# Inputs asked for three units ahead, the routing bias ahead of them, and the last tile scaled on ScalarE

## The chip, the cores and the metric

The kernel runs on one core of a Trainium2 chip. The metric is the device time of one execution in microseconds (us). Before the change the median of three runs is 327.57 us (327.46 to 328.42).

## What is computed

Two stages follow each other: a linear attention with decay (RWKV) over 4 sequences of 768 steps with 8 heads of 48, and on its output a mixture of 8 experts that sends each of the 3072 rows to the one expert with the highest gate.

```python
for t in range(S):                       # attention, per batch and head
    cur = einsum('bhd,bhe->bhde', u * kt, vt)
    y[:, :, t] = einsum('bhd,bhde->bhe', rt, state + cur)
    state = wt[..., None] * state + einsum('bhd,bhe->bhde', kt, vt)

x = y as [3072, 384]                     # mixture of experts
logits = x @ w_gate + modality_bias[modality_id]
e = argmax(logits); gate = softmax(logits)[e]
out[row] = gate * (relu(x[row] @ w1[e]) @ w2[e])
```

## The kernel before, in words

The 3072 steps are cut into 24 units of 128 steps. The loop `for i in range(-2, NU)` (L1044) is a software pipeline over them: iteration `i` of `att_iter` (L400) prepares unit `a = i+2` (decay scans and the scaling of keys and receptances on VectorE), multiplies unit `m = i+1` (scores, key turn, state update on TensorE) and writes the output of unit `z = i`. GpSimd works one unit further ahead: in iteration `i` it makes the decays, the products r*k and the within-unit products (`decays`, `keys`, `within`, L320 to L337) of unit `i+3`, and then a share of `dV` of unit `i`. From iteration 15 on it also sends one finished row tile an iteration to the buffer `xs` in device memory (`scatter`, L834).

The inputs r, k, w of a unit lie in one of `NIN = 4` tiles `ins[n % 4]` (L106). `load(n, cuts, key)` (L130) asks for parts of unit n on SyncE's queue: k is the cut (512, 1024), w the cut (1024, LIN), r the cut (0, 512), of 256, 264 and 256 KB. With a key, the request also waits for the VectorE instruction recorded under it in `step`: ("second", i) is the second scan of iteration `i`, ("mask", i) the masking of the scores, ("first", i) the first scan. Before the change iteration `i` asks for unit `i+6` (L1071 to L1075). That unit goes into the tile of unit `i+2`, which the same iteration is still reading: k waits until VectorE has scaled the keys, w for the second scan, r until VectorE has scaled the receptances. After that comes `loadv(i + 3)`, which waits for the masking.

SyncE's queue is worked off in the order of the program. In iterations 18 to 23 it also holds zero fills of `xs` (`fill`, 386 KB each) and sixteen pieces of 192 KB of the first expert's weights (`w_raw` in parts of eight, EARLY); these are issued ahead of the unit requests of the same iteration. In iteration 0, `early()` (L215) asks for the routing's bias `bb` and the modality numbers `mi`; VectorE reads `bb` in `setup_a` (L230), which runs at the end of iteration 1. At the end of iteration 20 `blk_load(0)` (L856) asks for the rows of the first expert block in `xs`; it may only start when the scatters of units 0 to 5 have landed, of which the last is issued by GpSimd in iteration 20.

The expert stage then runs six blocks over TensorE (`blk_up`, `blk_down`). In the last block, tiles of 128 rows are scaled by the gate in `last_scale` (L962) and sent to the output by `last_out` (L970); the last tile is scaled by VectorE (L966), the one before by ScalarE (L968).

Of the kernel before, what the change touches and what calls it, by code (L numbers as in the profile page):

```python
# [13 lines left out]
AF = mybir.ActivationFunctionType  # L14
ALU = mybir.AluOpType
# [3 lines left out]
P = 128  # L19
# [3 lines left out]
DM = H * D  # L23
# [12 lines left out]
BT = WIDTH[-1]  # L36
# [19 lines left out]
LIN = 2 * 4 * P + WIN  # L56
# [26 lines left out]
def kernel(ctx: ExitStack, tc: tile.TileContext, rkw, vt, wf, cst, mid, wg, bias, w1, w2, out):  # L83
    nc = tc.nc
# [17 lines left out]
    BOTH = slice(0, 1), slice(1, 2)  # L102
    PREP = ("K", "G")
    WORK = ("R", "A", "W", "dT", "v", "wx")
    NIN = 4
    ins = [pa.tile([P, WO + WIN], F32, name=f"in{i}", bufs=1) for i in range(NIN)]  # L106
    pw = [pa.tile([P, 4 * SEG], F32, name=f"pw{i}", bufs=1) for i in range(NPW)]
    KT = wk.tile([P, 2, 4, 64], F32, name="KT", bufs=1)
    T = {}

    def wt(n, tag, sh, bufs=None, dt=F32):
        T[tag, n] = (pa if tag in PREP else wk if tag in WORK else rt).tile(sh, dt, tag=tag, name=f"{tag}{n}", bufs=bufs)
        return T[tag, n]
# [5 lines left out]
    step = {}  # L119
# [5 lines left out]
    def behind(dma, key):  # L125

        if key in step:
            after(dma, step[key])

    def load(n, cuts=((0, 512), (512, LIN)), key=None):  # L130
        for c0, c1 in cuts:
            o = KO - 512 if c0 else RO
            behind(nc.sync.dma_start(out=ins[n % NIN][:, o + c0:o + c1], in_=rkw[n, :, c0:c1]), key)

    def r_of(n):
        return ins[n % NIN][:, RO:RO + 512]

    def k_of(n):
        return ins[n % NIN][:, KO:KO + 512]

    def w_of(n):
        return ins[n % NIN][:, WO:WO + WIN].rearrange("p (a c b) -> p a c b", a=4, c=2)[:, :, :, 0:P // 2]

    def loadv(n, key=None):
        behind(nc.sync.dma_start(out=wt(n, "v", [P, DM], 4), in_=vt[n * P:(n + 1) * P, :]), key)
# [120 lines left out]
    def fill(j):  # L266
        n = BW // P // len(FILL)
        r = DUMMY + j * n * P
        ins = nc.sync.dma_start(out=xs[r:r + n * P, :].rearrange("(j p) c -> p j c", p=P), in_=zt[:, None, :].to_broadcast([P, n, XW]))
        rows_apart("xs", ins)  # L270
        return ins
# [59 lines left out]
    def within(n, *parts):  # L331
        t, o, l = ins[n % NIN], RO + P // 2, KO - RO - P // 2
        if n in APARTS and ("wx", n) not in T:
            wt(n, "wx", [P, 2, 4, P // 2], 2)
        for ks in parts:
            v = t[:, o:o + 2 * l].rearrange("p (k x) -> p k x", k=2)[:, ks, 0:512 - P // 2].rearrange("p k (c j) -> p k c j", j=P // 2)[:, :, ::2]
            nc.gpsimd.tensor_tensor(out=T["wx", n][:, ks] if n in APARTS else v, in0=v, in1=w_of(n).rearrange("p a k j -> p k a j")[:, ks], op=ALU.mult)  # L337
# [6 lines left out]
    def spread(n, tag, src, c0, bufs=None):  # L344
        X = sides(wt(n, tag, [P, 4, P], bufs).rearrange("p a b -> p (a b)"))
        be, k, v = heads(BE1 if (n, tag) == (1, "K") else BE)[:, :, c0:c0 + P // 2], 1 if tag == "K" else 0, sides(src)
        if n == 0 or n in APARTS:
            w = T["wx", n][:, k] if n else sides((r_of, k_of)[k](NIN - 1))[:, :, 1 - k]
            nc.vector.tensor_tensor(out=X[:, :, k], in0=v[:, :, k], in1=be, op=ALU.mult)
            nc.vector.tensor_tensor(out=X[:, :, 1 - k], in0=w, in1=be, op=ALU.mult)  # L350
        else:
            nc.vector.tensor_tensor(out=X, in0=v, in1=be[:, :, None, :].to_broadcast([P, 4, 2, P // 2]), op=ALU.mult)

    def first(n):
        return n % NCH == 0
# [1 line left out]
    def ok(n):  # L357
        return 0 <= n < NU
# [41 lines left out]
    def att_iter(i):  # L400
        a, m, z = i + 2, i + 1, i
# [36 lines left out]
        if ok(a):  # L438
# [3 lines left out]
            pp, n, be = pw[a % NPW], 4 * SEG, BE1 if a == 1 else BE  # L442
# [5 lines left out]
        x_third(0)  # L448
        if ok(a):
            if a != 1:  # L450
                spread(a, "K", k_of(a), 3)
            nc.vector.reciprocal(out=pp[:, 1:n:SEG], in_=be[:, 2:n:SEG])
            nc.vector.tensor_copy(out=W, in_=be[:, 2:n:SEG])
            x_third(1)
# [4 lines left out]
        if ok(m):  # L459
            K, R, v = T["K", m], T["R", m], T["v", m]  # L460
# [28 lines left out]
        if ok(m):  # L489
            A = wt(m, "A", [P, 2, 4, P])  # L490
            pS = pq.tile([P, 2, 4, P], F32, tag="pS", name=f"pS_{m}")
            for p in range(4):
                for hh in range(2):
                    q = slice(64 * hh, 64 * hh + 64)
# [13 lines left out]
        if ok(m) and not last:  # L508
# [9 lines left out]
            for hh in range(2):  # L518
                q = slice(64 * hh, 64 * hh + 64)
# [4 lines left out]
        if ok(z):  # L524
            A, R, v = T["A", z], T["R", z], T["v", z]
# [47 lines left out]
    def x_third(k):  # L573
        if thirds:
            fn = thirds.pop(0)
            if fn:
                fn()
# [74 lines left out]
    def route_a(c):  # L652

        n = PART[c]
        sh = [P, n, E]
        lg, eq = logit_of(c), equal_of(c)
        if c:
            clear(c)
        nc.vector.scalar_tensor_tensor(out=lg, in0=rcol(FROM[c] * E, n, E), scalar=-1.0, in1=biasT[:, units(c)], op0=ALU.mult, op1=ALU.subtract)
        if c == 0:  # L660
            yield
        mx = wt(c, "mx", [P, NMOST], 1)[:, 0:n]
        nc.vector.tensor_reduce(out=mx, in_=lg, axis=AX.X, op=ALU.min)
        if c == 0:
            yield
        nc.vector.tensor_tensor(out=eq[:, :, 1:E + 1], in0=lg, in1=mx[:, :, None].to_broadcast(sh), op=ALU.is_equal)
        yield
        flat = lambda t: t[:, 0:n].rearrange("p a b -> p (a b)")
        nc.vector.tensor_tensor_scan(out=flat(seen), data0=flat(same), data1=eq.rearrange("p a b -> p (a b)"), initial=0.0, op0=ALU.mult, op1=ALU.max)
        if c == 0:  # L670
            yield
            nc.vector.tensor_tensor(out=lg, in0=lg, in1=mx[:, :, None].to_broadcast(sh), op=ALU.subtract)
            yield
        oh = T["oh", c] = wt(c, "oh", [P, NMOST, E], 2, BF16)[:, 0:n]
        nc.vector.tensor_tensor(out=oh, in0=eq[:, :, 1:E + 1], in1=seen[:, 0:n, 0:E], op=ALU.is_gt)
        yield
        if c:
            nc.vector.tensor_tensor(out=lg, in0=lg, in1=mx[:, :, None].to_broadcast(sh), op=ALU.subtract)
            with nc.allow_low_precision("whole numbers up to 10"):
                nc.vector.tensor_reduce(out=ohs, in_=T["oh", 0].rearrange("p a b -> p b a"), axis=AX.X, op=ALU.add)  # L680
        nc.gpsimd.tensor_copy(out=T["xp", c][:, :, DM + 1:DM + 2].bitcast(I32), in_=tidi[:, units(c), None])
        yield
# [157 lines left out]
    X, late = {}, []  # L840
# [120 lines left out]

    def last_scale(q, j):  # L962

        ot, y, g = T["xp", 1][:, j, 0:DM], X["y", q, j], X["xg", q][:, j, 0:1]
        if j == BT // P - 1:
            return nc.vector.tensor_scalar(out=ot, in0=y, scalar1=g, scalar2=None, op0=ALU.mult)  # L966
        else:
            nc.scalar.activation(out=ot, in_=y, func=AF.Copy, scale=g)  # L968

    def last_out(j):  # L970

# [68 lines left out]
    def hook_b(c):  # L1040
        route_b(c)
        pend.extend(range(FROM[c], FROM[c] + PART[c]))

    for i in range(-2, NU):  # L1044
        if i in EARLY:
            if i == EARLY[0]:
                e0 = nc.sync.value_load(e0i[0:1, 0:1], min_val=0, max_val=E - 1)
        if 1 <= i < 1 + len(SETUP):
            hooks.append(SETUP[i - 1])
        if i == PART[0] + 1:  # L1050
            ra, tb = route_a(0), table(0)
            hooks.extend([lambda: None] * 2 + [lambda: hook_b(0), lambda: [*tb]])
            slots[i + 1], slots[SCATTER] = [functools.partial(next, ra)] * 3, [functools.partial(next, ra)] * 2 + [lambda: [*ra]]
            slots[SCATTER + 1] = [functools.partial(place, 0, NEAR), functools.partial(gates_sum, 0), functools.partial(gates_put, 0)]
        if i == NU - 1:
            prep.close()
        att_iter(i)
        for n, at in enumerate(FILL):
            if i == at:
                behind(fill(n), ("first", i))  # L1060
        for n, at in enumerate(EARLY):
            if i == at:
                behind(w_raw(e0, n // FC, n % FC, parts=FC), ("first", i))
        apart = i >= APART
        if i >= -1 and ok(i + 3) and not apart:
            loadv(i + 3)
        if i == -2:
            load(3)
        if i == 0:
            early()  # L1070
        if ok(i + 2 + NIN):  # L1071
            load(i + 2 + NIN, ((512, 1024),))
            load(i + 2 + NIN, ((1024, LIN),), ("second", i) if apart else None)
        if ok(i + 2 + NIN):
            load(i + 2 + NIN, ((0, 512),))  # L1075
        if ok(i + 3) and apart:
            loadv(i + 3, ("mask", i))
        drain(DRAIN.get(i, 0))
        if i == LOAD:
            blk_load(0)  # L1080
# [308 lines left out]
```

## Time and profile before

| | us |
|---|---|
| median of three runs | 327.57 |
| the profiled execution | 327.71 |
| its span from the first to the last instruction | 325.9 |
| TensorE busy (matmul) in the span | 318.3 |
| VectorE busy | 236.4 |
| ScalarE busy | 203.2 |
| GpSimd busy | 151.5 |

Some 1.8 us of the execution lie outside the span. The attention stage takes the first 116 us, the experts the rest. PE is a matmul row, PEld a weight load, DVE is VectorE, ACT ScalarE, POOL GpSimd, and SPq SyncE's queue of requests. A row of a timeline gives start and duration in us, the line of the kernel, the operation, the tile written and the tiles read, the shape and the count of merged instructions; in brackets the idle time ahead of it and what ended it. Ends of matmuls are modelled, so pace is read from starts.

### The profile page before, as it was taken

How to read it: one execution, taken by the hardware profiler on the slowest of the kernel's cores; microseconds unless marked ns; L12 is line 12 of the kernel's file. 1: busy time of each engine (PE TensorE's matmuls, PEld its weight loads, DVE VectorE, ACT ScalarE, POOL GpSimd, SP SyncE). 2: the span in 40 equal slices, each digit the busy share in tenths (PEclk: the TensorE clock that was granted, in tenths of full speed). 3: DMA queues.
4: the chain of work that ended last, by engine and by line, in shares of the span. 5: the costliest groups of instructions: out<-in, count | busy, mean ns of one | idle time of the engine just before them, and what ended most of it. 6: DMA issues, size and time to landing. Idle time of an engine off the chain costs nothing. (4 is left out here: it accounts for less than half of the span.)

```text
span 325.9 us, 10298 instructions
## 1 busy us (share of the span) xinstructions
PE 318.3 (98%) x3913; PEld 296.4 (91%) x3913; DVE 236.4 (73%) x542; ACT 203.2 (62%) x503; POOL 151.5 (46%) x204
## 2 busy tenths in 40 slices
PE   7999999999999999999999999999999999999994
PEld 2789999999999988899889999999999988999984
DVE  7999999999999784794669668768258445915620
ACT  1586788697789894461469357856956944615420
POOL 5999999989996197055751300310210220121022
PEclk9999999999999999999999999999999999999998
DMA  7988777777887862516854800540640663310001
GB/s 257 388 283 266 235 225 225 237 224 228 263 270 233 205 200 91 105 73 236 291 179 105 263 24 2 138 154 2 129 185 2 191 156 99 97 73 22 1 33 56
DMA packets 39136, 52.51 MB, mean 161 GB/s; under 512 B 19205, under 2 KB 26149, under 8 KB 39076
## 3 DMA queue, kind: packets, MB, share of 16 engines
q1 hardware_dynamic: 35972, 42.28, 43.8%
q0 software_dynamic: 3104, 9.47, 7.7%
q8 instruction: 33, 0.54, 0.7%
q14 instruction: 27, 0.22, 0.2%
HBM read 55.63 MB, written 11.88 MB: 207 GB/s over the span
## 5 line engine op out<-in xcount | busy, mean ns | idle before, releaser
L948 POOL DMA_INDIRECT out<-ot,xg x23 | 25.3, 1101 | 127.2 <-ACT ot L947 125.1
L910 DVE SCALAR_TENSOR_TENSOR hl<-pS_u,hh 128x512 fp32r<-128x512 f32 (+2 forms) x40 | 25.0, 624 | 43.5 <-ACT hh L909 43.5
L317 DVE TENSOR_TENSOR wl<-raw,wh 128x768 fp32r<-128x768 f32 x52 | 48.8, 963 | 2.3 <-ACT wh L316 1.9
L316 ACT CAST wh<-raw 128x768 fp32r<-128x768 f32 (+1 forms) x60 | 44.9, 785 | 0.0
L905 PE MATMUL pS_u<-xh,wh 128*128 128x512 f32 (+2 forms) x120 | 44.0, 367 | 0.0
L909 ACT ACTIVATE hh<-pS_u 128x512 fp32r<-128x512 f32 (+2 forms) x40 | 21.8, 546 | 35.2 <-PE pS_u L905 35.2
L905 PE MATMUL pS_u<-xh,wl 128*128 128x512 f32 (+2 forms) x120 | 43.7, 364 | 0.0
L835 POOL DMA_INDIRECT xs<-xp,posT x24 | 26.3, 1096 | 21.3 <-DVE posT L718 18.1
L926 PE MATMUL pY_d<-wh,hh 128*128 128x384 f32 x104 | 35.1, 337 | 0.0
L926 PE MATMUL pY_d<-wh,hl 128*128 128x384 f32 x104 | 35.0, 336 | 0.0
L926 PE MATMUL pY_d<-wl,hh 128*128 128x384 f32 x104 | 34.9, 336 | 0.0
L378 DVE TENSOR_TENSOR_SCAN pX_s<-pw,pX_s 128x268 f32<-128x268 f32 x47 | 33.4, 711 | 0.2
L905 PE MATMUL pS_u<-xo,wh 128*128 128x512 f32 (+2 forms) x120 | 30.8, 365 | 0.0
L497 DVE TENSOR_TENSOR A<-pS,cs 128x1024 f32<-128x1024 f32 x24 | 29.2, 1218 | 0.6 <-PE pS L495 0.6
L495 PE MATMUL pS<-R,K 64*128 64x128 f32 x384 | 26.8, 279 | 0.9 <-DVE R L350 0.9
L407 ACT ACTIVATE dV<-v,dT 128x48 f32<-128x48 f32 x108 | 27.0, 325 | 0.0
L926 PE MATMUL pX_d<-wh,hh 128*128 128x384 f32 x80 | 27.0, 337 | 0.0
L926 PE MATMUL pX_d<-wh,hl 128*128 128x384 f32 x80 | 26.9, 336 | 0.0
L926 PE MATMUL pX_d<-wl,hh 128*128 128x384 f32 x80 | 26.9, 336 | 0.0
L326 POOL TENSOR_TENSOR G<-in 128x512 f32<-128x512 f32 x24 | 26.1, 1089 | 1.5 <-PE pR_x L364 0.6
L545 PE MATMUL pY<-v,A 128*64 128x48 f32 x736 | 25.6, 222 | 0.0
L495 PEld LDWEIGHTS pS<-R,K 64*128 64x128 f32 x384 | 23.5, 188 | 1.9 <-DVE R L350 1.4
(354 smaller groups left out, 764.3 us busy)
## 6 DMA issues: line engine op xcount, KB each, us to landing
raw<-w SPq DMA_DIRECT2D x24, 768.0 KB
in<-rkw SPq DMA_DIRECT2D x47, 256.0 KB
in<-rkw SPq DMA_DIRECT2D x23, 264.0 KB
v<-vt SPq DMA_DIRECT2D x24, 192.0 KB
wg<-wf SPq DMA_DIRECT2D x8, 576.0 KB
raw<-w SPq DMA_DIRECT2D x16, 192.0 KB
xq<-xs SPq DMA_DIRECT2D x12, 192.0 KB
xq<-xs SPq DMA_DIRECT2D x12, 144.0 KB
```

Source lines behind the costliest of these rows:

```text
L316: nc.scalar.copy(out=wh[k][:, sl], in_=raw[k][:, sl])
L317: (eng or (nc.vector, nc.gpsimd)[k]).tensor_tensor(out=wl[k][:, sl], in0=raw[k][:, sl], in1=wh[k][:, sl].bitcast(F32), op=ALU.subtract)
L326: nc.gpsimd.tensor_tensor(out=G, in0=r_of(n), in1=k_of(n), op=ALU.mult)
L378: return nc.vector.tensor_tensor_scan(out=be[:, ::way], data0=pp[:, ::way], data1=d1[:, ::way], initial=0.0, op0=ALU.mult, op1=ALU.max)
L407: nc.scalar.activation(out=dV[:, h], in_=v0[:, h], func=AF.Copy, scale=dT[:, h:h + 1])
L495: nc.tensor.matmul(out=pS[:, hh, p], lhsT=K[q, p], rhs=R[q, p], start=True, stop=True)
L497: step["mask", i] = nc.vector.tensor_tensor(out=a2(A), in0=a2(pS), in1=mask[:, None, :].to_broadcast([P, H, P]), op=ALU.mult)
L545: nc.tensor.matmul(out=pY[q:q + 64, h * D:(h + 1) * D], lhsT=A[:, hh, p, q:q + 64], rhs=v[:, h * D:(h + 1) * D], start=(first(z) and h == ...
L835: rows_apart("xs", nc.gpsimd.indirect_dma_start(out=xs[:, :], out_offset=bass.IndirectOffsetOnAxis(ap=posT[:, n:n + 1], axis=0), in_=T["xb ...
L905: nc.tensor.matmul(out=pp, lhsT=wsrc[0][:, g, c * P:(c + 1) * P], rhs=xsrc[:, c, 0:w], start=(n == 0), stop=(n == 3 * KC - 1))
L926: nc.tensor.matmul(out=X["y", q, j][0:r1 - r0], lhsT=hsrc[:, r0:r1], rhs=wsrc[1][:, f], start=(f == 0 and n == 0), stop=(f == FC - 1 and n ...
L948: ins = nc.gpsimd.indirect_dma_start(out=out[:, :], out_offset=bass.IndirectOffsetOnAxis(ap=xg[0:m, j, 1:2].bitcast(I32), axis=0), in_=ot[ ...
```

## The change

Three things change. (1) From unit 5 on, iteration `i` asks for unit `i+5` in place of `i+6`, so unit 4 is asked for by name in iteration -2 and iteration -1 asks for no unit. The four tiles stay, so the new unit goes into the tile of unit `i+1`, which iteration `i-1` has finished reading; k now waits for the recorded scaling of the keys of the same iteration (("keys", i), `spread` returns it), w for the second scan as before, r for nothing. (2) With that, unit 5 is asked for in iteration 0 behind `early()`, where before it was asked for in iteration -1, ahead of it. (3) `last_scale` uses ScalarE for every tile.

```diff
-    NIN = 4
+    NIN, LEAD = 4, 3
...
             if a != 1:
-                spread(a, "K", k_of(a), 3)
+                step["keys", i] = spread(a, "K", k_of(a), 3)
...
-        ot, y, g = T["xp", 1][:, j, 0:DM], X["y", q, j], X["xg", q][:, j, 0:1]
-        if j == BT // P - 1:
-            return nc.vector.tensor_scalar(out=ot, in0=y, scalar1=g, scalar2=None, op0=ALU.mult)
-        else:
-            nc.scalar.activation(out=ot, in_=y, func=AF.Copy, scale=g)
+        return nc.scalar.activation(out=T["xp", 1][:, j, 0:DM], in_=X["y", q, j], func=AF.Copy, scale=X["xg", q][:, j, 0:1])
...
         if i == -2:
             load(3)
+            load(4, ((512, 1024), (1024, LIN), (0, 512)))
         if i == 0:
             early()
-        if ok(i + 2 + NIN):
-            load(i + 2 + NIN, ((512, 1024),))
-            load(i + 2 + NIN, ((1024, LIN),), ("second", i) if apart else None)
-        if ok(i + 2 + NIN):
-            load(i + 2 + NIN, ((0, 512),))
+        if i >= 0 and ok(i + 2 + LEAD):
+            load(i + 2 + LEAD, ((512, 1024),), ("keys", i) if apart else None)
+            load(i + 2 + LEAD, ((1024, LIN),), ("second", i) if apart else None)
+            load(i + 2 + LEAD, ((0, 512),))
         if ok(i + 3) and apart:
             loadv(i + 3, ("mask", i))
```

## Rows read from the trace of the kernel before

**Rows 1.** Busy time by stretch (us from:to, length, engines, clock, DMA share, GB/s).
```profile
20.51:25.39 4.88, 4.75 (x126) 4.51 (x122) 4.61 (x14) 4.26 (x17) 4.32 (x8) 1.00 0.93 303
25.39:30.59 5.20, 4.86 (x125) 4.57 (x122) 4.91 (x12) 3.91 (x14) 4.93 (x11) 1.00 0.90 294
47.73:52.29 4.56, 4.56 (x127) 4.38 (x124) 4.56 (x11) 3.67 (x14) 4.56 (x8) 1.00 0.82 249
```

**Rows 2.** Timeline of TensorE around 29 us.
```profile
28.25 0.44 PE L534 MATMUL pY<-SPb,R 128*64 128x96 f32 x5
29.03 0.63 PE L534 MATMUL pY<-SPb,R 128*64 128x96 f32 x10 [0.34 <-issue]
```

**Rows 3.** Timeline of VectorE, its two waits in iterations 1 to 4.
```profile
20.78 0.17 DVE L230 TENSOR_REDUCE em<-bb 128x2 f32<-128x16 f32 x1 [0.52 <-DMA bb<-bias]
...
30.80 0.42 DVE L569 TENSOR_TENSOR xp<-pY,dV 128x256 f32<-128x256 f32 x1 [0.50 <-PE pY L545]
```

**Rows 4.** The page's DMA queues: packets, MB, share of 16 engines.
```profile
q8 instruction: 33, 0.54, 0.7%
```

**Rows 5.** SyncE's requests up to iteration 3.
```profile
0.71 2.29 SPq L133 DMA_DIRECT2D in<-rkw  x5
...
6.10 0.98 SPq L133 DMA_DIRECT2D in<-rkw  x2
...
14.75 0.33 SPq L216 DMA_DIRECT2D bb<-bias  x1
...
22.52 1.94 SPq L133 DMA_DIRECT2D in<-rkw  x3
...
26.83 2.06 SPq L133 DMA_DIRECT2D in<-rkw  x3
```

**Rows 6.** SyncE's requests in iterations 17, 18 and 20.
```profile
89.30 2.06 SPq L133 DMA_DIRECT2D in<-rkw  x3
...
94.10 1.52 SPq L311 DMA_DIRECT2D raw<-w  x1
...
106.71 3.02 SPq L862 DMA_DIRECT2D xq<-xs  x4
```

**Rows 7.** Busy time by stretch in iteration 17, columns as in Rows 1.
```profile
91.25:93.25 2.00, 2.00 (x59) 1.95 (x57) 2.00 (x4) 1.84 (x8) 1.83 (x3) 1.00 0.95 318
```

**Rows 8.** Timeline of GpSimd: a late input early on, unit 13, unit 23.
```profile
11.02 0.64 POOL L337 TENSOR_TENSOR wx<-in 128x256 f32<-128x256 f32 x1 [0.43 <-DMA in<-rkw]
...
56.05 1.09 POOL L337 TENSOR_TENSOR in<-in 128x512 f32<-128x512 f32 x1
...
98.20 0.64 POOL L322 TENSOR_TENSOR pw<-in 128x256 f32<-128x256 f32 x1
98.79 1.09 POOL L326 TENSOR_TENSOR G<-in 128x512 f32<-128x512 f32 x1
...
101.40 1.01 POOL L835 DMA_INDIRECT xs<-xp,posT  x1 [0.16 <-DVE pX_s L378]
```

**Rows 9.** VectorE scales the keys of unit 13.
```profile
61.62 0.69 DVE L352 TENSOR_TENSOR K<-in,pX_s 128x512 f32<-128x512 f32 x1
```

**Rows 10.** The scatter of 101.40 us, from issue to landing.
```profile
DMA to landing us min/median/max: 4.7/4.7/4.7
```

**Rows 11.** VectorE as the first expert block's rows arrive.
```profile
113.16 1.31 DVE L881 STREAM_TRANSPOSE xt<-xq 128x512 f32<-128x512 f32 x2 [0.36 <-DMA xq<-xs]
```

**Rows 12.** TensorE at the first expert matmul.
```profile
116.41 0.50 PE L905 MATMUL pS_u<-xh,wh 128*128 128x512 f32 x1
```

**Rows 13.** Waits from 110 to 130 us: total, times, longest.
```profile
PEld pS_u L905 <- DVE xo L891: 0.3, 1, 0.3
```

**Rows 14.** Timeline of the tail, VectorE and GpSimd, and ScalarE's tile before.
```profile
317.20 0.58 ACT L968 ACTIVATE xp<-pX_d,xg 128x384 f32<-128x384 f32 x1 [1.39 <-PE pX_d L926]
...
320.99 0.34 PE L926 MATMUL pU_d<-wh,hl 128*128 128x384 f32 x1
321.37 0.62 DVE L966 TENSOR_SCALAR xp<-pU_d,xg 128x384 f32<-128x384 f32 x1 [6.25 <-PE pU_d L926]
```

More of the change, by code (lines that the diff above doesn't have):

```diff
@@ L349, in spread @@
             nc.vector.tensor_tensor(out=X[:, :, k], in0=v[:, :, k], in1=be, op=ALU.mult)
-            nc.vector.tensor_tensor(out=X[:, :, 1 - k], in0=w, in1=be, op=ALU.mult)
+            return nc.vector.tensor_tensor(out=X[:, :, 1 - k], in0=w, in1=be, op=ALU.mult)
         else:
-            nc.vector.tensor_tensor(out=X, in0=v, in1=be[:, :, None, :].to_broadcast([P, 4, 2, P // 2]), op=ALU.mult)
+            return nc.vector.tensor_tensor(out=X, in0=v, in1=be[:, :, None, :].to_broadcast([P, 4, 2, P // 2]), op=ALU.mult)
     def first(n):
```

## The prediction

> **What bounds the kernel now.** I read the page's busy times first: TensorE's matmul row fills 318.3 of 325.9 us, so a change pays only where it takes a gap out of TensorE or moves the start of a stage. Then I read the attention stage, which is where the requests change, iteration by iteration. A steady iteration of TensorE takes 4.56 us from key turn to key turn, and VectorE is busy for the same 4.56 us [rows 1]: the two are balanced, and TensorE waits for almost nothing. Two iterations are longer, the one from 20.51 us (4.88) and the one from 25.39 us (5.20) [rows 1]. Against 4.56 they lose 0.32 and 0.64, together 0.96 us. In the second of them the gap stands inside one group of equal matmuls, 5 done, then 0.34 us without a release by any engine, then 10 more [rows 2]; that isn't a wait for data. The DMA share was 0.93 and 0.90 in these two and 0.82 in the steady one [rows 1]. In the first 30 us the requests are behind; that is the only place in the stage with such gaps.
>
> VectorE has a wait of its own there, 0.52 us for the routing's bias at 20.78, but at 30.80 it waits 0.50 us for TensorE again [rows 3]. Last I read two ends: the hand-over to the experts, where the first expert matmul starts at 116.41 [rows 12] with rows that VectorE turns from 113.16 on, after 0.36 us of waiting for their DMA [rows 11]; and the tail, where the last scaling follows the last matmul at once [rows 14].
>
> **The change part by part.** The profiled execution took 327.71 us (span 325.9), 0.14 above the median of 327.57; the sum is made against 327.71.
>
> *The bias.* It was asked for at 14.75 [rows 5] and waited for until 20.78 [rows 3]: 6.0 us. Moved ahead of the three requests of unit 5 it goes out some 2 us earlier, and is there before VectorE asks at 20.26. That takes 0.52 us out of VectorE. TensorE didn't wait for VectorE between there and 30.80, where VectorE waits for TensorE, so alone it is worth nothing: VectorE would wait 1.0 in place of 0.5. Its use is that VectorE can follow if TensorE gets earlier. If that cover is gone, it is worth at most 0.52. Unit 5's requests go behind two small ones and one v tile, still ahead of 14.75; GpSimd reads unit 5 in iteration 2, after VectorE's row at 20.78, and 6.0 is the longest landing in these rows, so I cost this at nothing.
>
> *One unit less in the crowded stretch.* Before, the requests of units 8 and 9 start at 22.52 and 26.83 [rows 5], each when the keys of that iteration are scaled. After, those moments carry units 7 and 8. From 20.51 to 30.59 the DMAs moved 4.88 x 303 + 5.20 x 294 = 3.0 MB [rows 1]; a unit is 776 KB, 0.79 MB. Without it 2.2 MB are left, 219 GB/s, below the 249 of the steady iteration, which has no gap. So I take both gaps out: -0.96. The bounds are 0 (they come from something else) and -0.96. VectorE can follow by 0.52 + 0.50 = 1.0.
>
> On what the gap is: the queue marked instruction moved 33 packets and 0.54 MB [rows 4]. The Trainium skill, page "Runtime: NRT & Kernel Launch", section "Instruction fetch mechanics", says that a sequencer streams its code in blocks of 16 KiB, 256 instructions, over a DMA queue of its own, and that crossing a boundary is mostly hidden. The trace agrees with the block (0.54 MB / 33 = 16.4 KB). By "mostly hidden" the gap would not be a fetch and the change would not touch it; that is the first rival below.
>
> *The lead in the middle.* Each unit is asked for one iteration, 4.56 us, later against its readers. The cover is GpSimd's lead. Example: unit 13 was read by GpSimd's within at 56.05 and by VectorE at 61.62 [rows 8, 9]; GpSimd is done with it at 57.14, 4.5 us early. A late input here eats GpSimd's lead and not TensorE's time. Cost 0; if the lead were used up, what is over 4.5 us.
>
> *The lead at the end.* From iteration 15 on GpSimd has one scatter more an iteration and little idle time, and here its time counts: the scatter at 101.40 [rows 8] takes 4.7 us to land [rows 10], at 106.1, and the request for the first block's rows goes out at 106.71 [rows 6]. Slack: 0.6 us. Unit 23, formerly asked for at 89.30, now comes behind iteration 18's zero fill and weight piece; the latter ends at 94.10 + 1.52 = 95.62 [rows 6]. With 2.29 / 5 = 0.46 us a request [rows 5], k goes out at 95.7, w at 96.1, r at 96.6, v behind them. GpSimd wants w at 98.20 (decays) and r at 98.79 (r*k) [rows 8]. Time from request to landing: near row, the burst of 91.25 to 93.25 at 318 GB/s [rows 7] carries w and r of the triple that began at 89.30 and whose last issue began at 91.0: 2.2 us. Far row, an input asked for second at 6.10 (6.56) [rows 5] was waited for until 11.02 [rows 8], 4.5 us, with the queues full. I take 2.6, near the first, as fill and weight piece are just ahead: w at 98.7, r at 99.2 to 99.5, so GpSimd is 0.4 to 1.0 late, say 0.9, and the block's rows are 0.9 - 0.6 = 0.3 late. They were already waited for (0.36 [rows 11], and 0.3 by TensorE for the last piece made of them [rows 13]), so all of it reaches TensorE: +0.3. Bounds: 2.2 us of landing gives 0; 4.5 gives w at 100.6, 2.4 late, +1.8.
>
> The Trainium skill, page "DMA: Bandwidth & Descriptors", section "Anatomy of one DMA", fits a DMA (of another issue path) by about 2.0 us plus bytes / 436 GB/s; by that, as an estimate, 264 KB take 2.6 us and the term would be 0 to 0.3. The near row agrees in size; no run here shows that path for these tiles.
>
> *The request queue.* SyncE gets the same number of requests. The three of iteration 18 push its v, the next fill and weight piece by some 0.4 us; v of iteration 19 waits for the masking anyway, so the push ends there. Cost 0.
>
> *The tail.* VectorE started 0.04 us after the modelled end of the last matmul (321.33) and took 0.62; ScalarE's like tile took 0.58 [rows 14] and began 0.03 after its matmul. ScalarE has nothing else then. -0.05, all on the path; bounds -0.1 and +0.1.
>
> Sum: -0.96 + 0.3 - 0.05 = -0.7, from 327.71 gives 327.0 us.
>
> **The rivals.**
>
> *The gaps stay.* Speaking for it: the first gap (20.51) begins while units 5 and 6 are still landing, which the change leaves alone; such a gap may also be hidden work of the sequencer. Against: no iteration at 0.82 has one. Then the bias is hidden, and the end of the stage costs 0 to 0.3: 327.71 - 0.05 + 0.15 = 327.8, within 327.4 to 328.2.
>
> *All of the gain and none of the cost.* If landing takes 2.2 us, unit 23 is in time; and if the first block's rows come earlier against TensorE, the 0.3 us that TensorE waited for their last piece go too: 327.71 - 0.96 - 0.05 - 0.3 = 326.4, within 326.2 to 326.7.
>
> *Unit 23 arrives too late (slower).* Place: GpSimd's decays and r*k of iteration 20. Between 93.5 and 100.5 the zero fills (0.79 MB), two weight pieces (0.39), two v tiles (0.39) and now unit 23 (0.79) want to move, with the scatters some 2.6 MB, 370 GB/s over 7 us against 318 in the busy burst [rows 7]. If landing takes as long as in the full queues, GpSimd is 2.4 us late or more, and the price is 1.8 us and up; it makes the kernel slower from a lateness of 0.6 + 0.96 = 1.6 us on, or from 0.6 if the gaps stay. 327.71 - 0.05 + 1.8 = 329.5 with the gaps, 328.5 without them; with new gaps in TensorE's stream by the full queues up to 0.5 more. Against: the stretch is short, and the requests are limited by what SyncE can issue.
>
> **How the numbers follow.** Chances: forecast (326.5 to 327.5) 0.40, gaps stay 0.22, all of the gain 0.21, unit 23 late 0.17. The likeliest gives 327.0. A measurement of this kernel can tell about 0.3% from no change, 0.98 us: faster means under 326.59, slower over 328.55. Faster: 0.19 of the third case and 0.05 of the first, 0.24. Slower: 0.14 of the last and 0.01 of the second, 0.15. Within: 0.61. The range, 326.3 to 328.6, leaves out the low end of the full gain (0.07) and the upper part of the late unit (0.12).
>
> **What would show it.** Right: the iterations of TensorE from 20 to 31 us last 4.56 each; no wait of VectorE for the bias; the scatter of iteration 20 and the block's request come about 0.6 and 0.9 us earlier than 101.40 and 106.71, the latter less if unit 23 is late; on GpSimd a DMA wait ahead of decays and r*k of unit 23 and nowhere with consequence before; the last scaling on ScalarE at 0.58. Wrong: gaps without a releaser still in iterations 2 and 3, or new ones near 100 us; DMA waits of GpSimd that add up over iterations 15 to 20; a wait of TensorE at its first expert matmul.

## The result: slower by 0.7%, and the profile after

The changed kernel takes 330.18 us (median of 8 runs, 328.75 to 331.34) against 327.62 for the kernel before on the same chip: a ratio of 1.0068, interval 1.0046 to 1.0091. The same kernel in a later comparison gave 1.0057 (1.0042 to 1.0073). The prediction was 327.0 within 326.3 to 328.6: wrong, and on the wrong side of no change.

The profiled execution took 330.17 us, span 328.4, which is 2.5 more than before. To see where, the start of one fixed group (L602, the key turn's second part) is compared unit by unit. Before, then after:

```profile
87.91 0.35 PE L602 MATMUL pK_('k', 18)_2153<-cs,xp 64*128 64x64 f32 x6
...
110.17 0.40 PE L602 MATMUL pK_('k', 23)_2723<-cs,xp 64*128 64x64 f32 x6
...
118.70 0.39 PE L905 MATMUL pS_u<-xh,wh 128*128 128x512 f32 x1
```

```profile
86.86 0.36 PE L602 MATMUL pK_('k', 18)_2150<-cs,xp 64*128 64x64 f32 x6
89.87 0.52 PE L607 MATMUL pR_x<-cs,xT 128*64 128x8 f32 x12 [0.63 <-ACT dT L366]
95.21 0.52 PE L607 MATMUL pR_x<-cs,xT 128*64 128x8 f32 x12 [0.59 <-ACT dT L366]
...
110.79 0.40 PE L602 MATMUL pK_('k', 23)_2723<-cs,xp 64*128 64x64 f32 x6
117.42 0.51 PE L905 MATMUL pS_u<-xh,wh 128*128 128x512 f32 x1 [0.33 <-ACT xh L889]
119.08 0.50 PE L905 MATMUL pS_u<-xh,wh 128*128 128x512 f32 x1 [0.33 <-ACT xh L889]
120.54 0.40 PE L905 MATMUL pS_u<-xh,wh 128*128 128x512 f32 x1
```

Unit 18 is 1.05 us earlier than before, unit 23 is 0.62 later: 1.67 lost over iterations 17 to 21, 1.22 of it in the two waits for ScalarE's copy of line 366. The second group of expert matmuls (120.54, before 118.70) is 1.84 later: another 1.22 lost at the hand-over. 0.32 follow up to the last matmul and 0.34 behind it. -1.05 + 1.67 + 1.22 + 0.32 + 0.34 = 2.5.

The gain of 1.05 is where it was expected, though not by the change, as the tail alone shows below. The two iterations that lasted 4.88 and 5.20 us [rows 1] are regular now, and the DMA share fell (columns: stretch, its length, busy us of PE, PEld, DVE, ACT, POOL, clock, DMA share, GB/s):

```profile
20.39:24.97 4.58, 4.58 (x126) 4.40 (x123) 4.41 (x13) 3.97 (x16) 4.27 (x9) 1.00 0.69 192
24.97:29.53 4.56, 4.56 (x127) 4.38 (x124) 4.56 (x11) 3.68 (x14) 4.41 (x9) 1.00 0.83 243
```

The loss begins on GpSimd. Its timeline from iteration 15 on, with the scatters and the waits for inputs:

```profile
78.47 1.22 POOL L835 DMA_INDIRECT xs<-xp,posT  x1 [0.17 <-issue]
...
85.58 1.09 POOL L326 TENSOR_TENSOR G<-in 128x512 f32<-128x512 f32 x1 [0.60 <-DMA in<-rkw]
...
90.94 1.09 POOL L326 TENSOR_TENSOR G<-in 128x512 f32<-128x512 f32 x1 [1.05 <-DMA in<-rkw]
...
100.88 0.63 POOL L322 TENSOR_TENSOR pw<-in 128x256 f32<-128x256 f32 x1 [2.06 <-DMA in<-rkw]
102.31 1.09 POOL L326 TENSOR_TENSOR G<-in 128x512 f32<-128x512 f32 x1 [0.80 <-PE pK_('k', 21)_2501 L602]
...
104.92 1.01 POOL L835 DMA_INDIRECT xs<-xp,posT  x1 [0.16 <-issue]
```

These are units 20 and 21, where the product r*k waits for r, the third of its unit's requests, and unit 23, where the decays wait for w: 3.71 us of waiting for inputs. The sixth scatter goes out at 104.92, 3.5 later than before [rows 8], though the first was 0.9 earlier. What hangs on it, SyncE's requests (unit 23's w as a row of its own, the block's rows) and VectorE's first turn of these rows:

```profile
95.22 0.42 SPq L133 DMA_DIRECT2D in<-rkw  x1
```

```profile
108.51 2.83 SPq L862 DMA_DIRECT2D xq<-xs  x4
```

```profile
116.01 1.30 DVE L881 STREAM_TRANSPOSE xt<-xq 128x512 f32<-128x512 f32 x2 [2.59 <-DMA xq<-xs]
```

The block is asked for 1.80 later than before [rows 6]; VectorE waits 2.59 us for it where it waited 0.36 [rows 11] and starts 2.85 later; through ScalarE's copies (L889) TensorE's first group is cut up twice. From the request for w at 95.22 to the end of the wait at 100.88 are 5.7 us; the time from a request until its data is there is called its landing below. The tail is as expected: ScalarE's last scaling takes 0.58 [rows 14]:

```profile
323.52 0.58 ACT L964 ACTIVATE xp<-pU_d,xg 128x384 f32<-128x384 f32 x1 [3.58 <-PE pU_d L926]
```

### The profile page after: what moved, and what is told of

Its sections match the earlier page's. It is cut to its first block, busy times and chain, and to the rows that moved or that the text cites. A ratio compares the mean times of both kernels' runs of the same rounds, so it can differ in the third digit from the quotient of the medians.

```text
span 328.4 us, 10298 instructions
## 1 busy us (share of the span) xinstructions
PE 319.4 (97%) x3913; PEld 296.1 (90%) x3913; DVE 234.5 (71%) x541; ACT 204.3 (62%) x504; POOL 150.7 (46%) x204
## 5 line engine op out<-in xcount | busy, mean ns | idle before, releaser
L495 PE MATMUL pS<-R,K 64*128 64x128 f32 x384 | 26.8, 279 | 0.5 <-DVE R L350 0.5
L905 PEld LDWEIGHTS pS_u<-xh,wh 128*128 128x128 f32 x120 | 22.5, 188 | 3.7 <-ACT xh L889 1.5
```

The costliest lines, as they stand in the source:

```text
L495: nc.tensor.matmul(out=pS[:, hh, p], lhsT=K[q, p], rhs=R[q, p], start=True, stop=True)
L905: nc.tensor.matmul(out=pp, lhsT=wsrc[0][:, g, c * P:(c + 1) * P], rhs=xsrc[:, c, 0:w], start=(n == 0), stop=(n == 3 * KC - 1))
```

## The experiments

### The parts alone

The tail alone: the kernel before with ScalarE for every last tile.

```diff
...
-        if j == BT // P - 1:
-            return nc.vector.tensor_scalar(out=ot, in0=y, scalar1=g, scalar2=None, op0=ALU.mult)
...
+        return nc.scalar.activation(out=T["xp", 1][:, j, 0:DM], in_=X["y", q, j], func=AF.Copy, scale=X["xg", q][:, j, 0:1])
```

> The kernel before with only the last tile's scaling moved to ScalarE. Theory (late inputs on GpSimd cost the change its time): the tail is worth -0.05 us, so 327.5 to 327.7, and the stretch from the last matmul's start to the end of the span stays at 4.9 us, as before. Rival (the new tail costs time, since the changed kernel's stretch from there on was 5.25 us against 4.91): 0.3 us slower, about 327.9.

Measured: 327.75 us (12 runs), ratio 1.0006 (0.9996 to 1.0015). The tail is worth nothing that can be measured: from the start of the last matmul to the end of the span are 5.29 us here, 4.91 in the kernel before, and 4.90 in the catch-up kernel below, which has the new tail too. The surprise is at the other end. This kernel asks for its inputs as the kernel before does, and has no early gap. TensorE's key turns of units 3 and 4 and its next group:

```profile
20.34 0.46 PE L468 MATMUL pK_('k', 3)_511<-cs,K 64*128 64x64 f32 x8
24.92 0.46 PE L468 MATMUL pK_('k', 4)_629<-cs,K 64*128 64x64 f32 x8
29.48 0.40 PE L602 MATMUL pK_('k', 5)_742<-cs,xp 64*128 64x64 f32 x6
```

4.58 and 4.56 us, as after the change; 29.48 is 1.11 earlier than the 30.59 of before [rows 1]. Of the eight profiles in this study with four units of lead in the first iterations, two show the early loss (before, and the bias alone), six don't (0.88 to 1.11 earlier at this point). Nor do three units of lead prevent it: from the key turn of unit 3 to L602 of unit 5, where e.g. the profile after takes 9.14 us, the one before takes 0.94 more, and four of the seven profiles with three units of lead there take 0.29 to 0.53 more. The kernel with the six scatters together (below) has the gap at the very place of [rows 2]:

```profile
28.63 0.63 PE L534 MATMUL pY<-SPb,R 128*64 128x96 f32 x10 [0.24 <-issue]
```

So the 0.96 of the prediction was read from an execution that had it by chance.

The bias alone: asked for ahead of unit 5, all else as before.

```diff
-        if i == 0:
+        if i == -1:
             early()
```

> The kernel before with only the bias and the modality numbers asked for in iteration -1, ahead of unit 5; units are still asked for four ahead. Theory: VectorE's 0.52 us wait goes, TensorE's two long iterations of 4.88 and 5.20 us stay, time 327.6 +- 0.2. Rival (the bias alone makes the early iterations short): both iterations 4.56 to 4.6 us and the time 326.6.

Measured: 327.85 us, ratio 0.9996 (0.9977 to 1.0016): moving the request is worth nothing, as the prediction costed it. But the wait itself was chance too: in the six profiles without the early loss, which ask for the bias as before, VectorE reads it at 20.01 to 20.21 without a wait. So no run here tells what the 0.52 us cost the execution that had them. There they may have reached TensorE, against the prediction: VectorE's L569 came late, and TensorE's L534, which writes anew the tile pY that L569 reads, started 0.14 us after L569 had ended:

```profile
23.24 0.28 DVE L569 TENSOR_TENSOR xp<-pY,dV 128x128 f32<-128x128 f32 x1
```

```profile
23.66 0.88 PE L534 MATMUL pY<-SPb,R 128*64 128x96 f32 x16
```

In the tail alone the two start at 22.71 and 23.21.

### Where the loss comes from

A catch-up: the change, but iteration 6 asks for two units and from then on it is four ahead again.

```diff
-    NIN, LEAD = 4, 3
+    NIN, CATCH = 4, 6
...
-        if i >= 0 and ok(i + 2 + LEAD):
+        for u in () if i < 0 else (i + 5,) if i < CATCH else (i + 5, i + 6) if i == CATCH else (i + 6,):
+            if ok(u):
...
```

> The changed kernel, but in iteration 6 two units are asked for (11 and 12) and from then on a unit comes four ahead again, so units 12 to 23 are asked for as early as before. Theory: TensorE keeps the 1.06 us gained by 30 us, GpSimd has no DMA wait after iteration 14, the first expert matmul comes at 115.35 to 115.5, time 326.4 to 326.8. Rival (the loss comes from the changed order of requests and the tail, not from the late inputs): above 328.5 again, with TensorE waiting near 90 and 95 us.

Measured: 327.34 us (12 runs), ratio 0.9994 (0.9984 to 1.0003). The loss is gone. GpSimd waits for no input after iteration 14, its sixth scatter goes out at 100.47, and TensorE has no gap in the second half of the stage. So the loss lies in the requests after iteration 6. The reverse: the kernel before, with only units 20 to 23 three ahead.

```diff
-        if ok(i + 2 + NIN):
+        u = i + 6 if i < 14 else i + 5 if i > 14 else NU
+        if ok(u):
+            load(u, ((512, 1024),), ("keys", i) if i > 14 else None)
...
```

> The kernel before, with only units 20 to 23 asked for three ahead (iteration 14 asks for none). Bias, early units and tail are as before. Theory (these four units are the whole loss): 329.5 to 330.5, GpSimd waits for inputs in iterations 17, 18 or 20, the first block's rows are asked for after 108 us. Rival (the loss needs the shift of the earlier units or the new tail too): under 328.5.

Measured: 330.0 us (6 runs), ratio 1.0101 (1.0066 to 1.0136). The whole loss is there, from four late units. GpSimd waits in it as in the changed kernel (2.16 us for unit 20, 1.69 for unit 23), and TensorE has two gaps that no engine ends (gaps without a releaser, `issue` in the rows). TensorE in iterations 20 and 21:

```profile
100.80 0.44 PE L495 MATMUL pS<-R,K 64*128 64x128 f32 x4
101.87 0.94 PE L495 MATMUL pS<-R,K 64*128 64x128 f32 x12 [0.63 <-issue]
...
106.25 0.77 PE L495 MATMUL pS<-R,K 64*128 64x128 f32 x9
107.94 0.71 PE L495 MATMUL pS<-R,K 64*128 64x128 f32 x7 [0.91 <-issue]
```

Next, which of the four. Unit 23 alone late, behind the fill and the weight piece, which is the prediction's own place; and units 20 to 22 late with unit 23 in time:

```diff
...
+        u = i + 6 if i < 17 else i + 5 if i > 17 else NU
...
```

```diff
...
+        for u in (i + 6,) if i < 14 else (i + 5,) * (i > 14) if i < 17 else (i + 5, i + 6) if i == 17 else ():
...
```

> The kernel before, with one unit late: units 5 to 22 are asked for four ahead as before, unit 23 one iteration later, in iteration 18, behind the zero fill and the weight piece. Theory A (the lateness of unit 23 alone, as the prediction had it, only mis-sized): GpSimd waits 1.5 to 2.1 us for w of unit 23 in iteration 20, the first block's rows are asked for 1.5 us or more later than in the kernel before, and the time is 329.0 to 330.2. Theory B (the loss needs all of units 20 to 23: GpSimd is late from iteration 16 on and the lateness adds up): the wait for unit 23 is there, but part of it is taken by GpSimd's lead, and the time is 327.8 to 328.9. A gap of TensorE without a releaser near 102 or 108 us would say that the queues, not GpSimd, carry the loss.

> The kernel before, with units 20, 21 and 22 asked for three ahead and unit 23 four ahead, in the same iteration as unit 22 (17). Theory A (unit 23 alone carries it): GpSimd waits some 0.6 to 2 us in iterations 16 to 18 but has caught up by iteration 20; time 327.5 to 328.2. Theory B (the lateness of units 20 to 22 counts as well): GpSimd's waits of iterations 16 and 17 push the scatters by 1 us or more and the time is 328.5 to 330.

Measured: unit 23 alone 328.09 us, ratio 1.0022 (1.0001 to 1.0044); the other three 328.89, ratio 1.0044 (1.0022 to 1.0067). Both times lie where theory B put them. Unit 23 alone costs less than the change; for the other three the interval reaches up to the change's own 1.0057 and 1.0068, so that they cost less is not shown. GpSimd in the first:

```profile
100.02 0.63 POOL L322 TENSOR_TENSOR pw<-in 128x256 f32<-128x256 f32 x1 [2.79 <-DMA in<-rkw]
103.32 1.01 POOL L835 DMA_INDIRECT xs<-xp,posT  x1 [0.15 <-issue]
```

The wait is there, 2.79 us, yet this execution (327.4 us, 0.7 under the median of its kernel) hands over as early as the catch-up kernel does: the rows asked for at 106.81 still arrived in time for TensorE. So a late unit 23 seems to cost little until GpSimd is late already. In the second, TensorE has three gaps without a releaser, 0.47, 0.54 and 0.30 us:

```profile
91.58 0.44 PE L545 MATMUL pY<-v,A 128*64 128x48 f32 x8 [0.47 <-issue]
...
97.04 0.27 PE L602 MATMUL pK_('k', 20)_2386<-cs,xp 64*128 64x64 f32 x1 [0.54 <-issue]
```

### What crowds the stretch

Unit 23 ahead of the fill and the weight piece of iteration 18, the rest as changed:

```diff
...
+        if i == 18:
+            ask(i)
...
-        if i >= 0 and ok(i + 2 + LEAD):
+        if 0 <= i < 18:
+            ask(i)
```

> The changed kernel with unit 23's three requests ahead of iteration 18's zero fill and weight piece instead of behind them. Theory (units 20, 21 and 23 are late, each by itself): the waits of GpSimd in iterations 17 and 18 (0.6 and 1.05 us) and TensorE's loss of 1.6 us near 90 and 95 us stay; the wait of 2.06 us in iteration 20 falls under 1 us, the first block's rows come some 1.2 us earlier, time 328.9 to 329.5. Rival (unit 23 behind the fill, as I predicted, is the whole of it): 327.3 or less.

Measured: 329.81 us (6 runs), ratio 1.0063 (1.0041 to 1.0085). GpSimd no longer waits for unit 23, and nothing is gained: the DMA share of 95 to 110 us is 0.86 (0.70 before, 0.77 after), and TensorE has gaps, two at the same places of L495 as above and a third:

```profile
102.07 0.94 PE L495 MATMUL pS<-R,K 64*128 64x128 f32 x12 [0.48 <-issue]
...
108.13 0.71 PE L495 MATMUL pS<-R,K 64*128 64x128 f32 x7 [0.91 <-issue]
...
113.98 0.45 PE L364 MATMUL pR_x<-cs,G 128*64 128x2 f32 x9 [0.51 <-issue]
```

So the order of the queue isn't the point. Whether the bytes in the stretch are, the next run asks: the fills out of the stretch, the rest as changed:

```diff
-FILL = (18, 19)
+FILL = (8, 9)
```

> The changed kernel with the two zero fills (386 KB each) issued in iterations 8 and 9 instead of 18 and 19. Theory A (the stretch from 93 to 105 us is too full once unit 23 is in it too): its DMA share falls back under 0.85, unit 23 lands before GpSimd wants it or under 0.7 us late, the gap of 0.17 and later ones in TensorE's stream go, time 328.0 to 328.8 (1.2 to 2 us of the 2.5 back). Theory B (every unit asked for three ahead is late as soon as scatters run, from iteration 15 on, by its landing time alone): GpSimd's waits in iterations 17 and 18 stay at 0.6 to 1.6 us and the time at 329.5 or more.

Measured: 328.56 us (12 runs), ratio 1.0033 (1.0015 to 1.0051): half of the loss is gone, the time of theory A. In the profile, the slowest of the twelve executions (330.8 us), GpSimd doesn't wait for unit 23; it still waits 0.81 us in iteration 17, as theory B has it. And trouble moved with the fills. TensorE, and the stretch ahead of its first gap:

```profile
54.20 0.72 PE L495 MATMUL pS<-R,K 64*128 64x128 f32 x9 [0.74 <-issue]
...
60.06 0.46 PE L364 MATMUL pR_x<-cs,G 128*64 128x2 f32 x11 [0.62 <-issue]
```

```profile
49.00:54.00 5.00, 4.45 (x120) 4.09 (x117) 4.67 (x12) 3.92 (x14) 4.09 (x6) 1.00 0.93 288
```

All six scatters at the end of iteration 20, the rest as changed (one execution):

```diff
-        drain(DRAIN.get(i, 0))
+        drain(NEAR if i == max(DRAIN) else 0)
```

> The changed kernel with the six scatters of iterations 15 to 20 issued together at the end of iteration 20. Theory: without scatters beside them units 20 to 22 land in time, so GpSimd has no DMA wait in iterations 16 to 19; the block's rows come later, since six scatters of 1.0 to 1.2 us stand ahead of them, so the time is above 331. Rival (scatters have no part in the late landings): waits of 0.6 us or more in iterations 17 and 18, as in the changed kernel.

Measured: 337.53 us; the six stand in a row ahead of the hand-over, and the first expert matmul comes 6.9 us later than before. What it tells is the landing without scatters. SyncE's request for w of unit 21 and GpSimd's wait for it:

```profile
85.66 0.33 SPq L133 DMA_DIRECT2D in<-rkw  x1
```

```profile
89.20 0.64 POOL L322 TENSOR_TENSOR pw<-in 128x256 f32<-128x256 f32 x1 [1.27 <-DMA in<-rkw]
```

From the request to the end of the wait are 3.5 us (DMA share 0.77 from 83 to 90). The theory, that without scatters units 20 to 22 land in time, fails: GpSimd waits 0.82, 1.27 and 1.29 us for them. For unit 23 the scatters seem to matter: its w takes 3.5 us here, and 4.5 to 5.7 in the six profiles that have scatters and this unit behind fill and weight piece. In either case landing takes more than the 2.6 us assumed. Last, two units of lead (one execution):

```diff
-    NIN, LEAD = 4, 3
+    NIN, LEAD = 4, 2
...
-        if i >= 0 and ok(i + 2 + LEAD):
+        if i >= 1 and ok(i + 2 + LEAD):
```

> The changed kernel with units asked for two ahead (unit 5 in iteration 1): now GpSimd waits for inputs in every iteration, and the end of each wait shows a landing. Theory: before iteration 15 w lands 2.2 to 3 us after its request, from iteration 15 on, with the scatters, 4 to 5.5 us; the time is over 335. Rival (landing takes as long without scatters): 4 us and more from iteration 5 on.

Measured: 342.52 us. It shows landing in the quiet middle of the stage, though GpSimd doesn't wait in every iteration, as was expected. SyncE's request for w of one unit and GpSimd's wait for it:

```profile
43.05 0.33 SPq L133 DMA_DIRECT2D in<-rkw  x1
```

```profile
46.55 0.64 POOL L322 TENSOR_TENSOR pw<-in 128x256 f32<-128x256 f32 x1 [0.62 <-DMA in<-rkw]
```

3.5 us again (share 0.65 from 42 to 47). The five such waits from 31 to 71 us end 3.5 to 5.2 us after their requests, over the 2.2 to 3 of the theory. Waits single out the late loads; the packed traces also hold the semaphore events by which every request reports its landing. By these, in the profile after, w lands 2.8 to 4.3 us after each request made from 31 to 90 us, and 5.6 after that of unit 23. In the profile before, w of unit 23, asked for at 90.27, took 3.7 and its r, asked for at 91.04, 5.1.

### What the gaps without a releaser are

Count from the first gap of the kernel with only units 20 to 23 late (after 4 of 16 of L495) to the second (after 9 of 16): 12 + 16 + 16 + 12 + 16 + 32 + 8 + 6 + 9 = 127 matmul records, each with its weight load, and two semaphore instructions: 256 instructions. Counted in the same way, every such gap of 0.2 us or more in these traces, the one at 29 us before [rows 2] included, lies a multiple of 256 from the others, give or take three. The test makes the stream longer at its beginning:

```diff
-        for i in range(n):
-            nc.tensor.matmul(out=T["R"][:, 0:C_D], lhsT=wm[:, 0:P], rhs=wm[:, 0:C_D], start=(i == 0), stop=(i == n - 1))
+        for c, i in ((slice(j * C_D // k, (j + 1) * C_D // k), i) for k in (3 if n == NWARM[0] else 1,) for j in range(k) for i in range(n)):
+            nc.tensor.matmul(out=T["R"][:, c], lhsT=wm[:, 0:P], rhs=wm[:, c], start=(i == 0), stop=(i == n - 1))
```

> The kernel with only units 20 to 23 three ahead, whose TensorE stream is made 44 instructions longer in the first microseconds: each of the first 11 warm-up matmuls of 504 columns is cut into three of 168. In the same kernel without that, TensorE stopped without a releaser after 4 of the 16 matmuls of L495 of unit 21 and after 9 of the 16 of unit 22, and these two places are 256 instructions of its stream apart, as are all such gaps in the other traces. Theory F (a gap is a code block that comes late while the DMAs are full): the places move back by 44 instructions, to 4 matmuls before the end of the L545 group ahead of unit 21's key turn and to after the first matmul of the L468 group of unit 22, or to a multiple of 256 instructions from these; nothing is left at the old places. Theory W (a wait for data that the profile doesn't name): the gaps stay inside L495 of units 21 and 22. Time about 330 in either.

TensorE around its two gaps:

```profile
99.16 0.97 PE L545 MATMUL pY<-v,A 128*64 128x48 f32 x28
101.40 0.32 PE L545 MATMUL pY<-v,A 128*64 128x48 f32 x4 [1.27 <-issue]
...
106.21 0.27 PE L468 MATMUL pK_('k', 22)_2651<-cs,K 64*128 64x64 f32 x1
106.86 0.46 PE L468 MATMUL pK_('k', 22)_2651<-cs,K 64*128 64x64 f32 x7 [0.38 <-issue]
```

Measured: 329.52 us, and both gaps stand at the very instruction foretold, 28 of 32 and 1 of 8; L495 is whole. A wait for data can't move like that. The packed traces hold what ends these gaps: the packets of the queue marked instruction [rows 4]. In the attention stage one of 16 KB comes to each 256 instructions of TensorE, and in all 21 such gaps (0.24 us and more) of the sixteen profiles TensorE goes on 1.0 to 1.6 us after such a packet has ended. In this kernel they end at 100.12 and 105.54, and TensorE goes on at 101.40 and 106.86. In the kernel before one ends at 27.76, and TensorE goes on at 29.03. The late packets started 1.8 to 3.7 us after TensorE had crossed into the block before; at the other crossings the median is 1.3. The Trainium skill, page "Runtime: NRT & Kernel Launch", section "Instruction fetch mechanics", has a sequencer stream its code in blocks of 256 instructions by DMA, the crossing mostly hidden. The block size agrees. The hiding fails here: up to 1.27 us.

With most of the gaps goes a full DMA system: the stretch 98 to 102 us has a DMA share of 1.00 in this kernel, against 0.80 before. It is neither enough nor always needed: the kernel with unit 23 alone late had 1.02 there and no gap, and a small gap (0.27 us at 43.40 in the kernel with early fills) followed a stretch at 0.81.

### A kernel that might have been better, and the changed one again

The kernel before with its fills in iterations 13 and 14, ahead of the scatters:

```diff
-FILL = (18, 19)
+FILL = (13, 14)
```

> The kernel before (four ahead), with the zero fills of iterations 18 and 19 in iterations 13 and 14, ahead of the scatters. If full DMAs late in the attention stage still cost the kernel before something (its hand-over waits 0.36 us for the rows' DMA, and GpSimd has little idle time there), the time falls to 326.6 to 327.3. If not, or if the fills (0.79 MB) make the requests of iterations 13 and 14 late in their turn, it stays at 327.4 to 328.2. A gap of TensorE without a releaser near 70 to 80 us would show the second.

Measured: 327.25 us, ratio 1.0002 (0.9982 to 1.0023). The number lies in the first range, but the kernel before ran at 327.01 on this chip, so nothing is gained: the second expectation. The share of 93 to 101 us falls from 0.84 to 0.49, and a gap, at 82 us and not at 70 to 80, comes up behind the new place of the fills. TensorE, and the stretch around it:

```profile
81.81 0.63 PE L534 MATMUL pY<-SPb,R 128*64 128x96 f32 x10 [0.35 <-issue]
```

```profile
75.00:82.00 7.00, 6.65 (x180) 6.25 (x180) 6.93 (x21) 5.53 (x22) 6.64 (x10) 1.00 0.95 308
```

No version of this study beats the kernel before. Open was still the pair of waits for line 366 in the profile after; so the changed kernel unaltered, and with a third buffer for dT:

```diff
-        nc.scalar.copy(out=wt(m, "dT", [P, 4, 2]), in_=pd)
+        nc.scalar.copy(out=wt(m, "dT", [P, 4, 2], 3), in_=pd)
```

> The changed kernel itself, unaltered. Its first profile had two waits of TensorE for ScalarE's copy of line 366 (0.63 and 0.59 us, in iterations 17 and 18) and no gap at a block of 256 instructions; the experiments with the same late requests had gaps at these blocks (0.3 to 1.3 us each) and not these waits. If both are chance effects of the same full queues, this execution shows another mixture: gaps at the blocks (after 24 of 32 of L545 of unit 18, after 5 of 6 of L602 of unit 20, after 4 of 16 of L495 of unit 21, after 9 of 16 of unit 22), waits for line 366, or both, and the waits of GpSimd for late inputs again in iterations 16 to 20; time 329 to 331. If the waits for line 366 belong to the program, they are there again in iterations 17 and 18 with 0.6 us each.

> The changed kernel with three buffers for the tile dT in place of two. Line 366's copy then waits for GpSimd's product dV of a unit one earlier, so that GpSimd's lateness can't hold it. If GpSimd's lateness held it in iterations 17 and 18, its lag behind TensorE's line 364 (0.9 us there, 0.1 elsewhere) is 0.1 in all iterations, and if nothing else takes its place the time falls by up to 1.2 us, to 329. If it was something else, lags of 0.4 us and more stay wherever TensorE's line 364 ends while GpSimd is in a scatter, and the time is 329.5 to 331.

Measured: 329.25 us, ratio 1.0057 (1.0042 to 1.0073), and 329.22, ratio 1.0055 (1.0039 to 1.0071). In neither did TensorE wait for line 366. GpSimd's waits are there again, and TensorE has gaps at the blocks instead. The unaltered kernel's GpSimd and TensorE:

```profile
86.30 1.09 POOL L326 TENSOR_TENSOR G<-in 128x512 f32<-128x512 f32 x1 [0.99 <-DMA in<-rkw]
...
90.90 1.09 POOL L326 TENSOR_TENSOR G<-in 128x512 f32<-128x512 f32 x1 [0.30 <-DMA in<-rkw]
...
99.28 0.63 POOL L322 TENSOR_TENSOR pw<-in 128x256 f32<-128x256 f32 x1 [0.52 <-DMA in<-rkw]
```

```profile
106.48 0.71 PE L495 MATMUL pS<-R,K 64*128 64x128 f32 x7 [0.38 <-issue]
```

From unit 18 to unit 23 this execution loses 0.76 us, the one with three buffers 1.68 (gaps of 0.39 and 0.64), the first profile 1.67. So the waits for line 366 are one chance form of the loss and not the loss. What held the copy there stays open: the third buffer says nothing, as the wait didn't come in either.

## Why the prediction was wrong, point by point

- **One unit less in the crowded stretch: -0.96.** The step failed. The rate fell as worked out (217 GB/s in mean from 20.39 to 29.53, against 219), but the rate was not the cause of the loss. The gap is a late code block that some executions have and some don't: six of eight profiles with the old early requests lack the loss, and four of seven with the new ones have part of it. That the first long iteration (0.32) was the bias wait passed on is likely and not shown. The rival "the gaps stay" had the right doubt, that it may be the sequencer's own work. The sentence on the skill then used "mostly hidden" as a reason that it is no fetch. The block size that it found in the same rows [rows 4] was the better clue.
- **The lead at the end: +0.3.** The place and the chain were right (GpSimd's decays and r*k, scatter, request, VectorE's turns, TensorE's first group), the size was wrong: landing was taken as 2.6 us from the bytes of one burst [rows 7], which doesn't say whose bytes they are; in that very execution w and r of the triple took 3.7 and 5.1, not 2.2. After the change it was 5.7 for w of unit 23, and 3.5 in the quiet middle. The far row, 4.5 [rows 8], was the nearer one. By the Trainium skill's page "DMA: Bandwidth & Descriptors", section "Anatomy of one DMA", whose fit is for another issue path, it would be 2.6 us, as an estimate. The runs show 2.8 to 5.7.
- **The lead in the middle: 0.** Right up to iteration 14 (one wait of 0.18 us), wrong for units 20 to 22, where GpSimd waits for inputs and its lead no longer covers them; that the scatters used it up is argued, not shown. These units were put under the same cover as unit 13, without rows of their own; late alone, they cost 0.44%.
- **"Unit 23 arrives too late (slower)", 0.17.** The rival that came nearest, at 328.5 to 329.5, with the full queues that it named. But unit 23 alone costs 0.22%. It is four late units that add up over iterations 17 to 20, the outcome listed under "wrong" as waits of GpSimd that add up. The half microsecond for new gaps was too small a term: TensorE lost 0.76 to 1.68 us between units 18 and 23 in the three profiles of the changed requests.
- **The bias 0, the request queue 0, the tail -0.05.** The bias wait, there by chance, is gone, and the moved request is worth 0.9996; ScalarE took 0.58 as said, worth 1.0006, both no change. For the queue no run speaks apart; unit 23 ahead of fill and weight piece won no time.

With the terms as they now stand, read from the results and so no forecast: early 0, tail 0, and from unit 18 to the last matmul 3.21, 2.19 and 1.84 us in the three profiles (the last with the third buffer), which from 327.6 gives 329.4 to 330.8. Measured were 330.18, 329.25 and 329.22.

## What to carry to other kernels

A gap without a releaser in one execution is to be weighed with a second execution before anything is built on it. How long a request takes to land is read as a pair, its own issue (not that of the first of its group) and its landing or the wait that it ended, never from a burst of bytes; and a lead is counted against it at the place where the reading engine has least slack, here GpSimd under the scatters. Where DMAs run at a share near 1, the engine with the longest code can stop for its own instructions, so moving bytes into such a stretch can cost even an engine that waits for none of them.

## What the runs showed of the hardware

- A load of 264 KB that SyncE asks for landed 2.8 to 4.3 us after its request between 31 and 90 us of the profile after, and 5.6 us after it in a stretch at a DMA share of 0.93 (98 to 102 us).
- TensorE's code arrives in blocks of 256 instructions, one 16 KB packet each. A crossing that came late cost 0.24 to 1.27 us, never showed as a wait for anything, and ended 1.0 to 1.6 us after its packet. The second of a pair can stand where the share is back near 0.6 (at 106 to 108 us), but its packet had been under way before: in the kernel with only units 20 to 23 late it started at 105.45, 3.6 us after the crossing before. What held it that long stays open.
